# Six units instead of five with combined blocks in both layers, and another order of the attention work, in a fused attention and mixer kernel

## The chip, the cores and the metric

The kernel runs on one core of a Trainium2 chip. The metric is the device time of one execution in microseconds (us): the median of three runs before the change.

## What is computed

Eight batches of cosine attention with 12 heads, 448 positions and 64 elements per head, and then a mixer on the result. In the reference, cut to what matters:

```python
q_n = q / (norm(q) + 1e-6);  k_n = k / (norm(k) + 1e-6)
attn = softmax(q_n @ k_n.T / tau)            # per batch and head, 448 x 448
x = (attn @ v), heads side by side           # 8 x 448 x 768
h = (x.T @ U @ V).T                          # U: 448 x 32, V: 32 x 448, over positions
u = x + h
out = u + relu(u @ w_ch1) @ w_ch2            # w_ch1: 768 x 3072, w_ch2: 3072 x 768
```

Inputs and output are float32; the matmuls are bf16.

## The kernel before

**Attention.** For each batch, q and k come in three thirds of four heads by DMAs that POOL issues (L588). For each half third an engine squares the elements (L636 on ACT, L638 on POOL, L640 on DVE), DVE sums the squares (L644), ACT and DVE make the inverse norm (L658 to L666), and a normalizing product writes q or k of a pair of heads into a buffer (L712). Which engine does this product is `POOL_XN` (L351): POOL for q of batches 2 to 7, DVE for the rest. From batch 2 on a DMA on SP's queue transposes it (L728) into one of the `qkT` buffers; in batches 0 and 1 PE transposes (L566). Scores are computed in bursts of three slots (L774). Six slots of two PSUM banks hold up to 128 keys of two heads each; the last 64 keys of four heads share one slot, with four matmuls on a quarter of the array each. `groups_of` (L1491) puts slots into bursts, and `LAST` (L353) says at which head pair each of a batch's three quarter slots is placed. ACT takes the exponential of a slot (L792; L787 for the first raw keys), PE multiplies by v with a column of ones (L819, "values"), and DVE divides into X (L850 and L851; L855 and L857 in the first batches).

**Low rank.** After a batch, PE projects X by U (L934) and multiplies by V (L987), DVE adds the result to X (L996), and SP stores it as u in DRAM (L1025).

**Mixer.** The 28 tiles of 128 rows of u go through both layers in units: one of three tiles and one of one tile, plain (L1372 and L1414), and then twelve units of two tiles. In these twelve, the second layer is done in seven products of half blocks instead of eight (`mlp_seven`, L1248; its matmuls are L1289, 84 per unit), with blocks of w_ch2 that `seven_weights` has combined once, and sums of relu blocks by DVE (L1232 to L1234, `last_sums` L1243). The first layer of a unit is plain (L1260, 144 matmuls of 256 columns) for the first `HALF` = 7 of the twelve. The other five use seven products there too (`up_seven`, L1122; L1153, 252 matmuls of 128 columns, 36 per product). They need combined rows of w_ch1 (`seven_rows`, L1098, by DVE at L1112 to L1115, three of each), one of which is written over w_ch1 itself, and combined columns of u (L1135 to L1138). The row combinations lie in buffers of the attention that are free by then: X, `attn`, one v buffer, the buffers of normalized q and k. `up_seven` takes its products in the order 1, 6, 2, 7, 5, 3, 4; ACT copies product 1 (L1190), DVE adds sums from PSUM (L1175), ACT or DVE applies relu (L1181, L1209). One of its partial sums, `z12`, lies in a part of X (L445), so the copy waits until u of the last batches is stored (`x_free`).

**What sets the order.** Nothing is scheduled by hand. Every step is an `Op` with an engine, an estimated duration, what it depends on, buffers that it takes and releases, and a priority; some streams keep their order. `Plan.run` (L196) is a list scheduler over these estimates, and its order of starts is the program's order on each engine; at run time the engines wait for semaphores alone. An `Op` with `port=True` on DVE or POOL is not planned to start while one with `port=True` runs on the other. PE has the attention streams ahead of the mixer, whose matmuls fill what is left. At L1599 to L1602 the bursts of batches 3 to 7 get extra dependencies: the first of a batch on the last values matmul of the batch before, the second on L987 of the batch before, the fourth and later on values of an earlier pair of their own batch. In batch 0, where the plan has a gap on PE, warm-up matmuls (L698) are put in.

## Time and profile before

| what | us |
|---|---|
| median of three runs (lowest, highest) | 553.93 (553.42, 554.13) |
| the profiled execution, its own time | 553.89 |
| its span in the profile | 552.1 |
| first mixer matmul (L1372) | 39.16 |
| projections (L934) of batches 2 to 7 begin | 146.16, 193.88, 240.88, 286.89, 335.73, 379.80 |
| first combined first layer (L1153) begins | 409.06 |
| last matmul begins | 547.5 |

TensorE is called PE, VectorE DVE, ScalarE ACT, GpSimd POOL and SyncE SP. A line number such as L1289 is that of the kernel before. Busy time is time with an instruction on the engine; the table of groups gives the mean duration of one instruction, and the idle time of its engine just before it. The stretches cut the span into pieces; the chain of waits goes back from the last instruction to what released each step. The granted clock of PE is full but for one stretch of 3.4 us from about 20.6 us on.

### The profile page before, as it was taken

The numbers are of one execution on the slowest core, as the hardware profiler recorded it, in microseconds if no ns is written. First come the engines' busy times: TensorE is split into PE (matmuls) and PEld (weight loads), VectorE is DVE, ScalarE is ACT, GpSimd is POOL, SyncE is SP. The second block draws the span as 40 slices with busy tenths as digits, with TensorE's granted clock in tenths as the row PEclk, the third lists the DMA queues.
The fourth block names the chain that finished last, engine by engine and source line by source line (L and its number), as shares of the span: only waits on it lengthen the run. The fifth ranks groups of instructions, "written<-read, shape, count | busy, mean of one in ns | idle before, by whom it ended". The sixth has DMA issues, their size and how long they took to land.

```text
span 552.1 us, 14798 instructions
## 1 busy us (share of the span) xinstructions
PE 542.2 (98%) x6085; PEld 390.2 (71%) x6086; DVE 435.1 (79%) x978; ACT 281.4 (51%) x458; POOL 184.0 (33%) x216
## 2 busy tenths in 40 slices
PE   8899999999999999999999999999999999999996
PEld 6565565577857857767767767767778787878784
DVE  8889969989978897798789859657658585858583
ACT  7875746475575656656745754743314141414140
POOL 8626235325533552851543381020101111111111
PEclk9899999999999999999999999999999999999999
DMA  9999999959586949977997494332231312121201
GB/s 147 200 206 144 204 204 148 205 96 139 75 175 108 136 80 172 118 121 160 100 159 135 73 147 102 71 59 60 63 87 31 87 30 87 32 86 30 87 4 57
DMA packets 142324, 61.08 MB, mean 111 GB/s; under 512 B 101008, under 2 KB 142256, under 8 KB 142256
## 3 DMA queue, kind: packets, MB, share of 16 engines
q0 software_dynamic: 72352, 25.73, 43.0%
q1 hardware_dynamic: 69904, 34.41, 29.0%
q8 instruction: 47, 0.77, 0.6%
q14 instruction: 21, 0.17, 0.1%
HBM read 56.93 MB, written 15.93 MB: 132 GB/s over the span
## 4 chain that ended last, share of the span: by engine, by line
PE 91%; DVE 6%; ACT 1%; issue 1%; DMA 1%; DVEq 0%
PE bank L1289 30%; PE bank L1260 20%; PE bank L1153 13%; PE bank L819 8%; PE bank L774 7%; PE bank L1372 6%; PE bank L1414 4%; DVE qk_all L712 2%; PE bank L987 1%; DVE ss L644 1%; ACT attn L787 1%; PE bank L566 1%; PE bank L934 1%; DVE X_sb L857 1%; DMA relu<-in_q_dram 1%
## 5 line engine op out<-in xcount | busy, mean ns | idle before, releaser
L792 ACT ACTIVATE attn<-bank 128x896 bf16<-128x896 f32 (+1 forms) x163 | 140.4, 916 | 44.3 <-PE bank L774 43.8
L1289 PEld LDWEIGHTS <-relu 128*128 128x128 bf16 x1008 | 95.7, 98 | 66.4 <-issue 7.1
L1260 PE MATMUL bank<-uT,w_sb 128*128 128x256 bf16 x1008 | 120.2, 273 | 0.0
L1260 PEld LDWEIGHTS <-w_sb 128*128 128x128 bf16 x1008 | 95.2, 98 | 20.0 <-issue 7.9
L1289 PE MATMUL bank<-w_sb,relu 128*128 128x384 bf16 x576 | 102.7, 326 | 0.0
L712 POOL TENSOR_TENSOR qk_all<-qk_all,inv 112x512 bf16<-112x512 bf16 x36 | 41.0, 1148 | 85.0 <-DMA sqk<-qk_all 39.0
L644 DVE TENSOR_REDUCE ss<-sqk 112x8 f32<-112x512 bf16 x96 | 62.5, 672 | 4.4 <-ACT sqk L636 4.1
L819 PEld LDWEIGHTS <-attn 128*128 128x128 bf16 (+1 forms) x1536 | 55.1, 98 | 7.7 <-issue 4.2
L819 PE MATMUL bank<-v_nat,attn 128*128 128x65 bf16 (+1 forms) x1536 | 58.1, 194 | 0.9 <-DVE X_sb L857 0.4
L1270 ACT ACTIVATE relu<-bank 128x512 bf16<-128x512 f32 x53 | 31.6, 597 | 44.0 <-PE bank L1260 43.8
L774 PE MATMUL bank<-sqk 64*128 64x448 bf16 (+1 forms) x384 | 48.8, 359 | 1.1 <-ACT sqk L1436 0.5
L636 ACT ACTIVATE sqk<-qk_all 112x512 bf16<-112x512 bf16 x56 | 33.8, 632 | 23.3 <-DVE ss L644 22.0
L712 DVE TENSOR_TENSOR qk_all<-qk_all,inv 112x512 bf16<-112x512 bf16 x57 | 45.4, 821 | 0.3
L1153 PEld LDWEIGHTS <-w_sb 128*128 128x128 bf16 x720 | 41.0, 98 | 0.6
L1314 POOL TENSOR_TENSOR relu<-relu,u_nat 128x384 f32<-128x384 f32 x8 | 9.5, 1182 | 91.4 <-ACT relu L1312 91.3
L1190 ACT COPY attn<-bank 128x512 f32<-128x512 f32 x15 | 8.8, 585 | 60.4 <-PE bank L1153 59.5
L611 POOL DMA_DIRECT2D v_nat<-in_v_dram x42 | 31.2, 748 | 15.1 <-DMA w_sb<-in_moe_w_ch_dram 11.8
L1372 PE MATMUL bank<-uT,w_sb 128*128 128x384 bf16 (+1 forms) x288 | 35.6, 273 | 0.0
L1414 PE MATMUL bank<-w_sb,relu 128*128 128x384 bf16 x192 | 35.3, 326 | 0.0
L851 DVE TENSOR_TENSOR X_sb<-bank,rd 128x256 bf16<-128x256 f32 x72 | 30.5, 424 | 2.5
L1307 DVE TENSOR_TENSOR O_sb<-bank,O_sb 128x384 f32<-128x384 f32 x35 | 19.2, 554 | 16.2 <-PE bank L1289 11.5
L1153 PE MATMUL bank<-uT,w_sb 128*128 128x128 bf16 x540 | 31.8, 219 | 0.0
(137 smaller groups left out, 820.0 us busy)
## 6 DMA issues: line engine op xcount, KB each, us to landing
qk_all<-in_q_dram POOLq DMA_DIRECT2D x23, 224.0 KB, 4.4
qk_all<-in_k_dram POOLq DMA_DIRECT2D x23, 224.0 KB, 6.5
u_nat<-u SPq DMA_DIRECT2D x25, 192.0 KB, 2.8
w_sb<-in_moe_w_ch_dram POOLq DMA_DIRECT2D x4, 1152.0 KB, 17.7
w_sb<-in_moe_w_ch_dram POOLq DMA_DIRECT2D x8, 576.0 KB, 15.8
u<-X_sb SPq DMA_DIRECT2D x22, 192.0 KB, 4.7
v_nat<-in_v_dram POOLq DMA_DIRECT2D x11, 168.0 KB, 7.8
out_dram<-O_sb SPq DMA_DIRECT2D x12, 144.0 KB, 2.1
```

The source lines that it names most:

```text
L636: nc.scalar.activation(out=y, in_=x, func=AF.Square)
L644: lambda i=i, a0=a0, a1=a1, sq=sq: nc.vector.reduce_sum(ss.tile[:, i, a0:a1, :].rearrange("p h c -> p (h c)"), sq.tile[:, 0:a1 - a0, :].re ...
L712: (nc.gpsimd if pool_ else nc.vector).tensor_mul(dst, src, sc)
L774: nc.tensor.matmul(out=out, lhsT=qkT.tile.rearrange("p b s -> p (b s)")[r, n0:n0 + w], rhs=qkT.tile[r, SC:2 * SC, :].rearrange("p c s -> p ...
L792: exps.append(plan.add(Op("ACT", act_t(2 * S, 0.08), lambda sc=sc, c=c, attn=attn: nc.scalar.activation(out=attn.tile[:, :, off:off + S] i ...
L819: nc.tensor.matmul(out=av.tile[:, t, 0:D + 1], lhsT=tail.tile[:, hh, 128 * t:128 * (t + 1)] if tail and j == SC - 1 else (attn if j < SC - ...
L1153: o = plan.add(Op("PE", pe_t(128), lambda i=i, j=j, jj=jj: nc.tensor.matmul(out=mm.tile[:, 128 * jj:128 * jj + 128], lhsT=left[k](i, j), r ...
L1260: o = plan.add(Op("PE", pe_t(256), lambda j=j, e=e, cc=cc, mm=mm: nc.tensor.matmul(out=mm.tile[:, 256 * e:256 * e + 256], lhsT=w1_sb[:, cc ...
L1270: nc.scalar.activation(out=dst, in_=mm.tile[:, 0:512], func=AF.Relu)
L1289: o = plan.add(Op("PE", pe_t(CH), lambda j=j: nc.tensor.matmul(out=mm.tile[:, 0:CH], lhsT=left[k](j), rhs=right[k](j), start=(first and j ...
L1372: o = plan.add(Op("PE", pe_t(n), lambda cc=cc: nc.tensor.matmul(out=mm.tile[:, m:m + n], lhsT=w1_sb[:, cc, f * 128:(f + 1) * 128], rhs=uT. ...
L1414: nc.tensor.matmul(out=mm.tile[:, 0:c1 - c0], lhsT=relu.tile[:, f, i * 128:(i + 1) * 128], rhs=w2_t[:, f, c0:c1], start=(f == 0), stop=(f ...
```

## The change

- `HALF` is 6: the seventh of the twelve units does its first layer in seven products too, so six units do so.
- `LAST` has one placing for all batches from 2 on: a batch's three quarter slots go to head pairs 0, 2 and 4, so that three bursts hold one each. Before, batches 3 to 7 had two in the first burst and one in another.
- The first and second bursts of batches 4 to 7 have no extra dependency; batch 3 keeps them.
- q of batches 5 to 7 is normalized on DVE instead of POOL. Every normalizing product on DVE is now `port=True`, and the estimates of POOL's squares and products are 1.02 and 1.05 instead of 1.3 and 1.2.
- One of the twelve row combinations of w_ch1 (the third `S4`) goes to POOL.
- `z12` lies in `qkT` buffers instead of X. The copy of product 1 waits for the last values of batch 7, and the sum into `z12` for batch 7's last burst; neither waits for the stores of u.

The order in which the instructions stand after the change has 1512 matmuls at L1153 (1260 before), 864 at L1260 (1008), 147 warm-up matmuls (142), and otherwise the same matmuls. Normalizing products: 76 on DVE (58 before), 18 on POOL (36). ACT has 6 squares fewer and 4 relus of L1270 fewer, DVE 6 squares more and 8 relus of L1272 fewer. The diff, cut to its core:

```diff
-    HALF = 7
-    POOL_XN = {x: (0,) for x in range(2, B)}
+    HALF = 6
+    POOL_XN = {2:(0,),3:(0,),4:(0,)}
-    LAST = {0: 0, 2: 2, 4: 4}, {0: 0, 2: 0, 4: 4}
+    LAST = {0: 0, 2: 2, 4: 4}
...
-    xs, vs_ = X_t.bitcast(FP), v_t[1].rearrange("p h c d -> p (h c d)").bitcast(FP)
+    zs, vs_ = sqk_t[:, 3 * SQ + 2 * 2 * SC * SCH:].bitcast(FP), v_t[1].rearrange("p h c d -> p (h c d)").bitcast(FP)
-    r_z12 = fixed_ring([xs[:, 512 * i:512 * (i + 1)] for i in range(3, 6)])
+    r_z12 = fixed_ring([zs[:, 512 * i:512 * (i + 1)] for i in range(3)])
...
+    pool_s = plan.stream("POOL")
...
-                o = Op(on, 1.3 if on == "POOL" else 0.48 if on == "ACT" else 0.44, None,
+                o = Op(on, 1.02 if on == "POOL" else 0.48 if on == "ACT" else 0.44, None,
...
-            return plan.add(Op("POOL" if pool_ else "DVE", 1.2 if pool_ else dve_t(512), fn, deps=[deps[i]], acq=[xn],
-                               rel=[getattr(ld, "slot", ld), inv], prio=pr, port=pool_), pool_x if pool_ else None)
+            return plan.add(Op("POOL" if pool_ else "DVE", 1.05 if pool_ else dve_t(512), fn, deps=[deps[i]], acq=[xn],
+                               rel=[getattr(ld, "slot", ld), inv], prio=pr, port=True), pool_x if pool_ else None)
...
-        def rows_(f, deps, prio=2.5):
-            return plan.add(Op("DVE", 0.15 + N * 0.00053, f, deps=deps, prio=prio, port=True))
+        def rows_(f, deps, prio=2.5, eng="DVE"):
+            e = nc.gpsimd if eng == "POOL" else nc.vector
+            return plan.add(Op(eng, N * 0.00203 if eng == "POOL" else 0.15 + N * 0.00053, lambda: f(e), deps=deps, prio=prio,
+                               port=True), pool_s if eng == "POOL" else None)
-            a = rows_(lambda o=S1[i], x=A21, y=A22: nc.vector.tensor_add(o, x, y), free[i])
-            c = rows_(lambda o=S2[i], x=S1[i], y=A11: nc.vector.tensor_sub(o, x, y), [a, *free[3 + i]])
-            d = rows_(lambda o=S4[i], x=A12, y=S2[i]: nc.vector.tensor_sub(o, x, y), [c, *free[2]], 3)
-            e = rows_(lambda o=A21, x=A11, y=A21: nc.vector.tensor_sub(o, x, y), [a, *after], 2.7)
+            a = rows_(lambda v, o=S1[i], x=A21, y=A22: v.tensor_add(o, x, y), free[i])
+            c = rows_(lambda v, o=S2[i], x=S1[i], y=A11: v.tensor_sub(o, x, y), [a, *free[3 + i]])
+            d = rows_(lambda v, o=S4[i], x=A12, y=S2[i]: v.tensor_sub(o, x, y), [c, *free[2]], 3, "POOL" if i in (2,) else "DVE")
+            e = rows_(lambda v, o=A21, x=A11, y=A21: v.tensor_sub(o, x, y), [a, *after], 2.7)
-    def up_seven(tiles, relu, tops, ready, left, made_by, qk_free, x_free):
+    def up_seven(tiles, relu, tops, ready, left, made_by, qk_free, s_free, z_free):
...
-                                 [o, *x_free], [s1[g]])
+                                 [o, *s_free], [s1[g]])
-                    x["z12"] = op("DVE", PS, sum_op(of(z12[g]), of(s1[g]), B_, False), [o, x["cp"]], [z12[g]])
+                    x["z12"] = op("DVE", PS, sum_op(of(z12[g]), of(s1[g]), B_, False), [o, x["cp"], *z_free], [z12[g]])
...
-                slots += [(x, SC - 1) for x, at in LAST[b > TB].items() if at == p]
+                slots += [(x, SC - 1) for x, at in LAST.items() if at == p]
...
-            up = *up, [o for p in range(NPAIR) for o in got[B - 1, p, "qkT"][1]], [o for t in range(7) for o in made[3, t]]
+            up = *up, [o for p in range(NPAIR) for o in got[B - 1, p, "qkT"][1]], [last_av[B - 1, p] for p in range(NPAIR)], bursts[B - 1][-1:]
-            o.deps += ([last_av[b - 1, NPAIR - 1]] if k == 0 else first_v[b - 1] if k == 1 else
-                       [last_av[b, k - 3]] if k > 2 else [])
+            o.deps += ([last_av[b, k - 3]] if k > 2 else [] if b > 3 else
+                       first_v[b - 1] if k == 1 else [last_av[b - 1, NPAIR - 1]] if k == 0 else [])
```

## The prediction

> **What bounds the kernel now.** I read the page first, then the stretches of 20 us, the chain of waits, the timelines of TensorE (PE) and VectorE (DVE), and last the order in which both programs' instructions stand.

> ```profile
> PE 542.2 (98%) x6085; PEld 390.2 (71%) x6086; DVE 435.1 (79%) x978; ACT 281.4 (51%) x458; POOL 184.0 (33%) x216
> ```
> PE is busy 98% of the span, but its ends are modelled, so the stretches must say where it loses time.

> ```profile
> 0.00:20.00 20.00, 16.72 (x179) 12.21 (x179) 16.79 (x43) 15.14 (x33) 16.87 (x25) 1.00 1.37 160
> 20.00:40.00 20.00, 18.92 (x295) 12.93 (x294) 17.17 (x58) 17.36 (x26) 7.15 (x10) 0.91 1.23 207
> ...
> 80.00:100.00 20.00, 19.04 (x177) 11.04 (x178) 16.41 (x35) 12.11 (x22) 12.13 (x15) 1.00 1.35 148
> ...
> 280.00:300.00 20.00, 20.00 (x201) 13.19 (x199) 18.50 (x39) 8.73 (x15) 7.21 (x8) 1.00 0.74 128
> ```
> The columns are PE, weight loads, DVE, ACT, POOL. PE idles in the first 40 us (batch 0), about 1 us near 95 us, and then hardly at all; DVE is the next engine, with up to 18.5 us of 20.

> ```profile
> 384.88 10.70 PE bank L1260 x98
> 395.58 13.65 PE bank L1289 x84
> 409.23 14.07 PE bank L1153 x252
> 423.30 13.65 PE bank L1289 x84
> ```
> This is the chain of waits: nothing but PE, and each unit's price can be read. A combined first layer (L1153) is 252 matmuls in 14.07 us, 55.8 ns each; a plain one (L1260) runs at 10.70/98 = 109.2 ns, so its 144 take 15.72 us; a second layer (L1289) takes 13.65 us. From 384.9 us to the last matmul at 547.8 us these pieces meet without a gap.

> [...] the normalizing product on DVE (L712) takes 0.68 us alone and up to 1.53 us beside one on POOL.

> **The change, part by part.**

> *A sixth combined unit.* The order shows 252 L1153 matmuls six times instead of five, and 144 L1260 fewer. 15.72 - 14.07 = 1.65 us less PE work, on the path. Added with it are 15 bank sums on DVE (L1175, 0.69 us) and 9 relus (L1181, 0.62) and 3 copies (L1190, 0.585) on ACT. Today's five such units hide the same work without a gap, so it costs 0; without that cover PE would wait for its banks.

> *Quarter-array slots.* A burst of scores is three slots. Timeline of PE:

> ```profile
> 340.96 0.86 PE L774 MATMUL bank<-sqk 64*128 64x448 bf16 x10
> 341.76 2.03 PE L1260 MATMUL bank<-uT,w_sb 128*128 128x256 bf16 x17
> ...
> 346.77 0.74 PE L774 MATMUL bank<-sqk 64*128 64x448 bf16 x6
> 347.45 1.26 PE L1260 MATMUL bank<-uT,w_sb 128*128 128x256 bf16 x10
> ```
> From its start to the next line's a mixed burst (10 matmuls, one half-array slot and two quarter ones) takes 0.80 us, an unmixed one (6) 0.68: 0.12 us for the change of tile, and the one with a single quarter slot (8 matmuls, 361.68 to 362.47) 0.79, so the price is per mixed burst. Batches 3 to 7 have two mixed bursts now and three after: 5 x 0.124 = +0.62 us, on the path.

> *Order of the work.* With the first bursts of batches 4 to 7 tied to nothing, the order puts two bursts of the next batch ahead of the projections of the one before. Counting units from 1, the last attention matmul stood just inside the seventh unit's first layer (378 us); now it stands 48 matmuls before the end of the sixth unit's second layer, 48 x 0.1625 = 7.8 us ahead of the first combined layer, which is the seventh unit's. This moves PE work, it removes none. Does a moved burst find its operands? They come by a transposing DMA on SP's queue (1.23 us to issue, 5.1 us median to landing, 8.5 at most). PE work that stands between such a DMA and the burst that reads it is at least 8.9 us before; after it is at least 9.7 (batch 2) and 12.3 for the others. I cost it at 0; without that cover, up to 8.5 us once per batch. SP's own queue has the same 36 transposes and stores in another order; nothing new waits there.

> *Row combinations ahead of the first combined unit.* They now follow the last attention closely. From its last matmul to the seventh unit's second product, the first to read a row combination, PE has 7.8 + projections 0.4 + eight L987 of 0.1625 (1.3) + the first product, 36 x 0.0558 (2.0) = 11.5 us. DVE's queue up to the last row sum that this product needs: two column sums (0.54), a head scaling (0.55), two row sums (2 x 0.87), a unit sum (0.475): 3.3 us, so 8 us of cover and a cost of 0. All that is queued on DVE in that stretch, with three more unit sums and two relu sums (3 x 0.475 + 2 x 0.47), eight additions to X (8 x 0.465) and two in-place row differences (2 x 0.87) comes to 3.3 + 7.8 = 11.1 us; the last of it is read by the fourth product, 4 us later. If DVE comes 5 us late there, PE waits some 0.5 us. One row difference (1536 columns) goes to POOL. No row shows it; the nearest, 512 columns on POOL in 1.04 us, gives an estimate of 3.1 us, from 1.04 (no dearer than 512) to 4.7 us (1.55 per 512 beside DVE). It is read by the sixth product, over 10 us after the unit begins: 0 at either end. The new homes only change what is waited for: ACT's copy L1190 waits for the last attention instead of the stores of u, DVE's first sum for the last burst. Both are over before the unit; behind them queue that unit's relus. Cost 0.

> *Normalizing products to DVE.* Batches 5 to 7: 18 products leave POOL (18 x 1.04 = 18.8 us) and join DVE. POOL's q and k loads then no longer stand behind them. On DVE records overlap:

> ```profile
> 249.37 1.47 DVE L996 TENSOR_TENSOR X_sb<-bank,X_sb 128x384 bf16<-128x384 f32 x3
> ...
> 251.70 1.26 DVE L644 TENSOR_REDUCE ss<-sqk 112x8 f32<-112x512 bf16 x2
> ```
> Two reductions of 0.67 us take 1.26, three additions of 0.54 take 1.47: each following one occupies 0.08 us less than its record. So a product occupies 0.60 us, 18 of them 10.8 us. Per stretch between the projections of one batch and the next (from the order's counts, records less 0.08 each): batch 3 to 4, DVE 37.4 us against 44.5 of PE; 4 to 5, 35.5 against 42.7; 5 to 6, 32.8 against 42.4. Today it is 34.4 of 47.0, 33.6 of 46.0, 35.9 of 48.8. DVE goes from 73% to 84%: hidden, if DVE can give up idle time. I take 0; unhidden, see the rival.

> *The start.* Correcting POOL's price for squares reorders batch 0. DVE now takes the last two squares' sums before it normalizes: the first normalizing product, at 17.17 today, must follow POOL's fourth square (ends 17.71) and one sum, to about 18.4. ACT then does four copies before its first wide exponential, so that starts at about 22.0 instead of 20.55.

> ```profile
> 20.55 1.72 ACT L792 ACTIVATE attn<-bank 112x896 bf16<-112x896 f32 x2
> 22.16 0.23 ACT L658 ACTIVATE ln<-ss 112x32 f32<-112x32 f32 x1
> 22.42 0.23 ACT L659 ACTIVATE ln<-ln 112x32 f32<-112x32 f32 x1
> 23.17 2.90 ACT L792 ACTIVATE attn<-bank 112x896 bf16<-112x896 f32 x3 [0.52 <-PE bank L774]
> 26.07 0.53 ACT L1436 COPY sqk<-bank 128x448 bf16<-128x448 bf16 x1
> ```
> But what interrupts the 16 exponentials today goes ahead of them or to DVE: two small ones with the wait behind them (23.17 - 22.16 = 1.0 us) and a copy (0.5); and the last two thirds' normalizing is over 3 us sooner, which frees the waits between 31 and 35 us (0.5). -2.0 + 1.4 = -0.6 us. Bounds: +1.4 if nothing is recovered, -1.5 if all waits go. The five more warm-up matmuls (142 to 147, 0.28 us) stand in waits. The waits near 92 to 102 us (0.70 us for DVE's X, some 1.7 with the smaller ones) stand in nearly the same order: 0, from -0.9 to +0.9.

> **Sum.** The profiled execution took 553.89 us: span 552.1 and 1.8 around it; it lies 0.04 under the median of 553.93. 553.89 - 1.65 + 0.62 - 0.6 = 552.26, so 552.3 us.

> **Rivals.**
> *The gain is spent at the edges* (no change): the start gives +0.4 instead of -0.6 and the first combined unit waits 0.5 us. For it: the saving on PE is 1.0 us net, no more than one wait, and the start's order is new. Against it: exponentials are what the start waits for, and ACT's stretch gets cleaner. 552.3 + 1.0 + 0.5 = 553.8 us.
> *DVE becomes the bound* (slower): from batch 3's projections to batch 6's PE waits for head scalings and normalizing. It decides from the point where DVE idles or is blocked over 44.5 - 37.4 = 7.1 us in the first stretch, 7.2 in the second, 9.6 in the third. Today that sum is 12.6 (47.0 - 34.4), of which 7.3 us is idle by the stretches[...]. If it keeps 9 us a stretch, PE loses 1.9 + 1.8 us: 552.3 + 3.7 = 556.0 us. For it: DVE's 18.5 of 20 us already today. Against it: the 18 products leave POOL, so POOL blocks less, and the idle is mostly lack of work.

> **How the numbers follow.** Forecast 552.3: 0.56, with its own range 550.8 to 552.8. No change, at 553.8: 0.23. DVE as the bound, at 556.0: 0.21. A measurement of this kernel can tell about 0.2%, 1.1 us, from no change. Faster 0.56, same 0.23, slower 0.21. The low end is the forecast with the start's and the 95 us stretch's better bounds taken partly (-0.9 and -0.6); the high end, 555.8, goes into the slow case until no more than 2 in 10 is left out.

> **What would show it.** L1153 x1512 and L1260 x864; mixed bursts of 8 matmuls only, three in each batch; 14.07 us before every second layer from the first combined unit on, with no gap ahead of it. DVE busy at 82 to 90% between the third and the sixth projections, with PE at 100% and no wait of PE for DVE, confirms the cover; PE waits for DVE's X or for bank releases there would make the slow rival right. The first MLP matmul (L1372), at 39.16 us today, should come near 38.6; later than 40 would refute my working of the start.

## The result, and the profile after

The changed kernel takes 552.95 us (median of 20 runs, 550.98 to 554.85) against 554.10 for the kernel before (20 runs, 553.29 to 555.12): a ratio of 0.9973, 95% interval 0.9965 to 0.9982, so faster by 0.27%. Its times lie in two groups, ten from 550.98 to 552.56 and ten from 553.35 to 554.85, and what parts them is the subject of half of what follows. The profiled execution below is of the slower group (its own time 553.73 us, span 551.9); a second one, of the faster group (551.07 us, span 549.3), is called the repeat.

Three lines of the kernel have new numbers that are needed here: the plain first layer L1260 is now L1263, the second layer L1289 is L1292, the combined first layer L1153 is L1156. The first line of the page after:

```profile
PE 540.4 (98%) x6199; PEld 389.2 (71%) x6199; DVE 448.3 (81%) x1009; ACT 284.1 (51%) x464; POOL 167.8 (30%) x199
```
PE is as full as before; DVE is busy 13 us longer. The same stretches of 20 us as in the prediction (PE, weight loads, DVE, ACT, POOL, then the granted clock):

```profile
0.00:20.00 20.00, 16.49 (x192) 12.13 (x193) 17.03 (x42) 15.36 (x34) 16.64 (x25) 1.00 1.38 163
20.00:40.00 20.00, 18.52 (x295) 12.42 (x293) 16.57 (x58) 17.63 (x27) 7.02 (x10) 1.00 1.23 207
80.00:100.00 20.00, 18.56 (x174) 10.80 (x173) 18.27 (x38) 11.68 (x22) 10.02 (x13) 1.00 1.33 139
280.00:300.00 20.00, 20.00 (x199) 12.46 (x197) 17.08 (x39) 11.90 (x20) 4.46 (x6) 1.00 0.92 145
```
Two things differ. Between 20 and 40 us the granted clock is 1.00, not 0.91. And between 80 and 100 us PE is busy 0.48 us less than before, with DVE nearly 2 us busier. In the repeat the same stretch has 19.88:

```profile
80.00:100.00 20.00, 19.88 (x185) 11.69 (x183) 18.20 (x43) 11.29 (x24) 11.95 (x15) 1.00 1.31 164
```
The chain of waits at the end of the kernel after:

```profile
381.35 14.07 PE bank L1156 x252
395.42 13.65 PE bank L1292 x84
409.07 14.07 PE bank L1156 x252
...
519.95 14.07 PE bank L1156 x252
534.02 13.66 PE bank L1292 x84
```
Six combined units, each 14.07 + 13.65 us, without a gap.

To see where the time went I split PE's way into four parts. A stall is what lies between the starts of two successive matmuls beyond the first one's price (55.8 ns for 128 columns, in proportion), where that is over 0.15 us; the rest is called work, small pauses included. All in us:

| | before | after | repeat |
|---|---|---|---|
| start of the first channel-mixing matmul (L1372, now L1375) | 39.16 | 38.25 | 37.33 |
| work from there to the first combined unit | 367.61 | 339.37 | 339.36 |
| stalls in that part | 2.29 | 3.57 | 1.83 |
| of these between 85 and 105 us | 1.77 | 2.00 | 0.28 |
| combined units, to the start of the last matmul | 138.44 | 166.16 | 166.16 |
| start of the last matmul (the sum) | 547.50 | 547.35 | 544.68 |

So against before: after has 0.91 less at the start, 0.52 less work (28.24 less, and one combined unit of 27.72 more) and 1.28 more stalls, 0.15 less in all; the repeat has 1.83, 0.53 and 0.46 less, 2.82 in all. The work is the same in both groups. They differ in the start, by 0.92, and near 90 us, by 1.72. Of the 0.92, 0.67 lie ahead of the first scores, which begin at 8.21 us in the kernel after and at 7.54 in the repeat (7.74 before).

Near 90 us the trace tells why. The batches are numbered from 0, so the third batch is batch 2. Timelines of DVE and then of POOL, kernel after:

```profile
87.42 3.61 DVE L713 TENSOR_TENSOR qk_all<-qk_all,inv 112x512 bf16<-112x512 bf16 x2
```
```profile
88.41 2.05 POOL L713 TENSOR_TENSOR qk_all<-qk_all,inv 112x512 bf16<-112x512 bf16 x2
```
The same two in the repeat:

```profile
86.61 1.28 DVE L713 TENSOR_TENSOR qk_all<-qk_all,inv 112x512 bf16<-112x512 bf16 x2
```
```profile
88.02 2.06 POOL L713 TENSOR_TENSOR qk_all<-qk_all,inv 112x512 bf16<-112x512 bf16 x2
```
These are normalizing products of the third batch, two on each engine. In the kernel after DVE's second one starts at 88.02 us and is still running when POOL starts its pair at 88.41; it ends only after that pair, having taken 3.01 us and not 0.68. In the repeat DVE is through 0.14 us before POOL starts. On DVE head scalings of batch 1 are queued behind these products. PE waits for them in the kernel after (first) and does not in the repeat (second):

```profile
90.67 1.62 PE L1417 MATMUL bank<-w_sb,relu 128*128 128x384 bf16 x9
93.73 0.65 PE L820 MATMUL bank<-v_nat,attn 128*128 128x65 bf16 x16 [1.44 <-DVE X_sb L858]
```
```profile
89.75 1.62 PE L1417 MATMUL bank<-w_sb,relu 128*128 128x384 bf16 x9
91.21 0.65 PE L820 MATMUL bank<-v_nat,attn 128*128 128x65 bf16 x16
```

### The profile page after: what moved, and what is told of

It is laid out like the page before. It is cut to its first block, busy times and chain, and to the rows that moved or that the text cites. A ratio compares the mean times of both kernels' runs of the same rounds, so it can differ in the third digit from the quotient of the medians.

```text
span 551.9 us, 15023 instructions
## 1 busy us (share of the span) xinstructions
PE 540.4 (98%) x6199; PEld 389.2 (71%) x6199; DVE 448.3 (81%) x1009; ACT 284.1 (51%) x464; POOL 167.8 (30%) x199
## 4 chain that ended last, share of the span: by engine, by line
PE 88%; DVE 8%; DMA 1%; issue 1%; POOL 1%; ACT 1%; DVEq 0%; POOLq 0%
PE bank L1292 29%; PE bank L1263 17%; PE bank L1156 15%; PE bank L820 8%; PE bank L775 7%; PE bank L1375 6%; PE bank L1417 3%; DVE ss L645 2%; DVE qk_all L713 2%; PE bank L988 1%; DMA qk_all<-in_k_dram 1%; DVE X_sb L997 1%; PE bank L935 1%; PE bank L567 1%; DVE X_sb L858 1%
## 5 line engine op out<-in xcount | busy, mean ns | idle before, releaser
L1292 PEld LDWEIGHTS <-relu 128*128 128x128 bf16 x1008 | 95.8, 98 | 66.5 <-issue 6.4
L1263 PE MATMUL bank<-uT,w_sb 128*128 128x256 bf16 x864 | 104.0, 273 | 0.0
L1292 PE MATMUL bank<-w_sb,relu 128*128 128x384 bf16 x576 | 102.9, 326 | 0.2 <-DVE relu L1246 0.2
L1263 PEld LDWEIGHTS <-w_sb 128*128 128x128 bf16 x864 | 81.6, 98 | 17.4 <-issue 7.0
L713 DVE TENSOR_TENSOR qk_all<-qk_all,inv 112x512 bf16<-112x512 bf16 x75 | 52.6, 727 | 0.2
L1273 ACT ACTIVATE relu<-bank 128x512 bf16<-128x512 f32 x49 | 29.2, 596 | 41.7 <-PE bank L1263 38.9
L1156 PEld LDWEIGHTS <-w_sb 128*128 128x128 bf16 x864 | 49.2, 98 | 0.8
L1193 ACT COPY attn<-bank 128x512 f32<-128x512 f32 x18 | 10.6, 586 | 67.6 <-PE bank L1156 66.6
L589 POOL DMA_DIRECT2D qk_all<-in_q_dram x24 | 17.8, 740 | 84.4 <-DVE qk_all L713 26.6
L637 ACT ACTIVATE sqk<-qk_all 112x512 bf16<-112x512 bf16 x50 | 30.1, 634 | 18.0 <-DVE ss L645 18.0
L1156 PE MATMUL bank<-uT,w_sb 128*128 128x128 bf16 x648 | 38.1, 219 | 0.0
L1184 ACT ACTIVATE relu<-relu 128x512 bf16<-128x512 bf16 x36 | 22.7, 630 | 29.8 <-DVE relu L1178 28.8
L1375 PE MATMUL bank<-uT,w_sb 128*128 128x384 bf16 (+1 forms) x288 | 35.6, 273 | 0.0
L713 POOL TENSOR_TENSOR qk_all<-qk_all,inv 112x512 bf16<-112x512 bf16 x18 | 20.0, 1120 | 39.7 <-DMA sqk<-qk_all 25.1
```

Of the source, the lines that this page charges most:

```text
L713: (nc.gpsimd if pool_ else nc.vector).tensor_mul(dst, src, sc)
L1156: o = plan.add(Op("PE", pe_t(128), lambda i=i, j=j, jj=jj: nc.tensor.matmul(out=mm.tile[:, 128 * jj:128 * jj + 128], lhsT=left[k](i, j), r ...
L1263: o = plan.add(Op("PE", pe_t(256), lambda j=j, e=e, cc=cc, mm=mm: nc.tensor.matmul(out=mm.tile[:, 256 * e:256 * e + 256], lhsT=w1_sb[:, cc ...
L1292: o = plan.add(Op("PE", pe_t(CH), lambda j=j: nc.tensor.matmul(out=mm.tile[:, 0:CH], lhsT=left[k](j), rhs=right[k](j), start=(first and j ...
L1375: o = plan.add(Op("PE", pe_t(n), lambda cc=cc: nc.tensor.matmul(out=mm.tile[:, m:m + n], lhsT=w1_sb[:, cc, f * 128:(f + 1) * 128], rhs=uT. ...
```

## The experiments

My theory after this: the sixth unit carries the gain; the other parts make room for it; and the two groups come from POOL's pair holding DVE's. Rivals: DVE's greater load is what costs; or the groups come from the first landings alone. The start was open: I took it to be the new price of POOL's squares.

**The changed kernel again**, as it is.

> The changed kernel once more, for a second profile. Its 20 times fall into two groups, 551.0 to 552.6 us and 553.3 to 554.9 us; the kernel before has one group. Theory 1 (DVE blocked by POOL): in the first profile the second of two normalizing products on DVE at 87.4 us was held for 2.9 us by two products of POOL, and PE then waited 1.6 us near 92 us; whether they meet depends on when POOL's DMAs let it go, so a profile of the fast group shows no long product there, a wait of PE under 0.5 us, and a time some 1.5 us lower. Theory 2 (the start): the groups come from the first 40 us, where PE's granted clock may or may not drop, and the wait near 92 us is the same in both.

551.64 us (9 runs, 551.06 to 554.16), ratio 0.9955, interval 0.994 to 0.997. Its profile is the repeat shown above: of the faster group, DVE's pair 1.28 us, no wait at 91 us. The blocking and the wait come and go together in these two profiles. The clock does not part the groups: in all 29 executions of the changed kernel, of either group, the mean granted clock is 0.998 or more, and 3.4 us at half clock would bring it to 0.997.

**Five combined units** and all else as changed.

```
-    HALF = 6
+    HALF = 7
```

> The changed kernel with the seventh unit's first layer plain again (HALF = 7), all else as changed: one part undone. My theory (the sixth combined unit is worth its PE work, 1.65 us, and nothing waits at it): 1.65 us slower than the changed kernel, 554.6 us, thus no faster than before. Rival (the gain of the change comes from the new order and the start, and the unit's saving is spent on waits for its row combinations): within 0.5 us of the changed kernel.

555.04 us (14 runs, 553.51 to 556.01), ratio 1.0008 (0.9995 to 1.0021): the whole gain is gone. Its times too fall in two groups, six from 553.51 to 554.40 us and eight from 555.03 to 556.01; by their middles, 553.6 and 555.4, each lies 1.7 us above the changed kernel's (551.9 and 553.7), which is the price of the unit. Its profile is of the slower group, with a stall of 1.80 us near 92 us, and shows one wait more. From the list of PE's waits:

```profile
PE bank L820 <- DVE X_sb L858: 2.3, 3, 1.6
...
PE bank L1292 <- DVE relu L1236: 0.7, 1, 0.7
```
The last line is a wait at 539.9 us, ahead of the last second layer. So the sixth unit carries the gain.

**The kernel before with a sixth combined unit** and nothing else.

```
-    HALF = 7
+    HALF = 6
```

> The kernel before with HALF = 6 alone: six combined units without the freed bursts, the spread slots and the new home of z12. My theory (the other parts are what makes the sixth unit possible: its rows and its buffers come free too late without them): PE waits at the first combined unit, whose first copy and product-6 sum wait for the stores of u of the last batch (DMA landing 2 to 5 us after the additions); 2 to 5 us lost there, 554.5 to 557.5 us. Rival (the unit alone carries the gain): 554.1 - 1.65 = 552.4 us, with no wait at its first combined layer.

557.85 us (6 runs, 557.39 to 559.34), ratio 1.0066 (1.0048 to 1.0084). Alone, the unit makes the kernel 3.7 us slower, since it now begins while batch 7 is still being added up:

```profile
PE bank L987 <- DVE X_sb L996: 1.3, 1, 1.3
...
PE bank L1289 <- DVE relu L1233: 0.8, 1, 0.8
PE bank L1153 <- DVE X_sb L996: 0.7, 1, 0.7
```
The wait that I expected, for the stores of u, is the smaller part: PE waits 0.60 us at 391.6 us behind a sum of DVE that itself waited 0.81 us for a store. The rest stands behind row sums and additions to X on DVE. The other parts of the change, together, are worth about nothing by themselves (the run before this one) and are what makes the unit worth something.

**The placing of the quarter-array slots back.**

```
-    LAST = {0: 0, 2: 2, 4: 4}
+    LAST = {0: 0, 2: 2, 4: 4}, {0: 0, 2: 0, 4: 4}
...
-                slots += [(x, SC - 1) for x, at in LAST.items() if at == p]
+                slots += [(x, SC - 1) for x, at in LAST[b > TB].items() if at == p]
```

> The changed kernel with the old placing of the quarter slots for batches 3 to 7: two mixed bursts per batch instead of three. On PE that is 5 x 0.124 = 0.62 us less. But the order then puts the last scores and values inside the first combined unit, whose rows need the buffers of the last values. My theory: PE waits 2 to 4 us there, 554 to 556.5 us; the new placing pays for itself by ending the attention sooner. Rival (the placing is only a cost of 0.62 us): 552.3 us.

556.24 us (7 runs, 554.86 to 557.56), ratio 1.0040 (1.0024 to 1.0056). The five mixed bursts that this spares are paid for dearly: the order now puts the last attention inside the first combined layer. Timeline of PE:

```profile
376.18 0.90 PE L775 MATMUL bank<-sqk 64*128 64x448 bf16 x6
377.63 0.49 PE L1156 MATMUL bank<-uT,w_sb 128*128 128x128 bf16 x6 [0.56 <-ACT attn L793]
...
382.39 1.03 PE L988 MATMUL bank<-A_sb,V_sb 128*128 128x384 bf16 x4 [0.43 <-ACT A_sb L1439]
384.23 0.23 PE L1156 MATMUL bank<-qk_all,attn 128*128 128x128 bf16 x1 [0.80 <-DVE attn L1116]
```
PE stalls some 4.4 us between 376 and 386 us, for attention, additions and row sums that the changed kernel has behind it by then. From 385.2 us on it then runs at half clock for 3.4 us, which comes on top (mean granted clock of the execution 0.997).

**POOL's old price for squares back.**

```
-                o = Op(on, 1.02 if on == "POOL" else 0.48 if on == "ACT" else 0.44, None,
+                o = Op(on, 1.3 if on == "POOL" else 0.48 if on == "ACT" else 0.44, None,
```

> The changed kernel with the old estimate of 1.3 us for POOL's squares, all else as changed: the reordering of batch 0 undone. My theory (the start is worth 0.6 us as predicted, 0.9 as profiled): the first mixer matmul comes at 39.1 us again, not at 38.2 or 37.5. With DVE that much later at 87 us its pair of products meets POOL's in every run, so 1.6 us more: 554.0 us, one group. The order also puts projections inside the first combined unit; if that unit waits for its rows, 1 to 3 us on top. Rival (the start's gain is absorbed before 100 us): 553.0 us, no different from the changed kernel.

554.77 us (19 runs, 553.76 to 556.01), ratio 1.0015 (1.0008 to 1.0022). The first mixing matmul came at 38.42 us and not at 39.1: most of the start is not the price's. From the first score it took 30.34 us, against 30.03 in the kernel after, 29.79 in the repeat and 31.42 before. This order has no wait of 1.6 us near 92 us, but three of 0.76 to 1.05 between 108 and 119. The start did not move as expected, and that led to the next two runs.

**The kernel before with eleven idle matmuls more.** The prediction's own line for 20 to 40 us had a granted clock of 0.91, and I had made nothing of it. Within it the kernel before has this stretch:

```profile
20.60:24.00 3.40, 3.35 (x42) 2.39 (x40) 2.48 (x8) 2.84 (x5) 2.84 (x4) 0.50 1.16 210
```
PE at half clock for 3.4 us. Ahead of it the kernel before leaves PE idle for 0.82 us at 17.5 to 18.3 us; the changed order has eleven idle matmuls just there. My guess was that the gap brings the half clock, so I put eleven into the kernel before:

```
...
+        if o.by == "PE" and scored[0] == 8:
+            warm_up(11)
+            scored[0] = 9
         if o.by == "PE" and not cool:
...
```

> The kernel before, unchanged but for eleven idle matmuls put into the gap that its PE leaves at 17.5 to 18.3 us, ahead of the key transposes. In its profile PE then ran at half the granted clock for 3.4 us from about 20.6 us; the changed kernel, which has eleven idle matmuls at that place by its planner's choice, shows the full clock throughout. Theory: the shorter start of the changed kernel is this clock, not the earlier squares. Then this kernel shows no stretch below full clock after 8 us, its first mixer matmul comes 1.0 to 1.5 us sooner after the first score than in the kernel before, and the whole takes 552.6 to 553.2 us (1.0 to 1.5 less than before). Rival: the start is bound by the engines that normalize (DVE, ACT), and the clock of PE does not matter: no more than 0.3 us change.

553.83 us (21 runs, 552.60 to 555.16), ratio 0.9992 (0.9985 to 0.9998). The first half came as expected. Timeline of PE, then the same stretch:

```profile
16.81 0.68 PE L776 MATMUL bank<-sqk 64*128 64x448 bf16 x2
17.41 0.79 PE L698 MATMUL bank<-warm 128*128 128x128 bf16 x11
18.30 0.37 PE L566 MATMUL bank<-ident,qk_all 112*128 112x112 bf16 x4
```
```profile
20.60:24.00 3.40, 3.30 (x65) 2.46 (x64) 3.33 (x11) 3.37 (x6) 2.58 (x4) 1.00 1.16 210
```
Full clock, 65 matmul records where there were 42, and from 13.8 us up to there the two traces agree within 0.03 us. From the first score to the first projection onto U takes 26.74 us, against 28.17 before. All 21 executions have a mean granted clock of 0.998 or more. The kernel before itself agrees: of 104 executions beside these experiments, 81 have 0.997 or less, and 16 have 0.999 or more, which leaves no room for such a stretch. These 16 are 0.5 us shorter by the medians (553.74 and 554.25 us). So the half clock comes in most executions of that order, not in all.

The second half of what I expected did not come: only 0.46 us of the 1.43 reached the end by the medians (and nothing in the profiled execution, 554.27 us, one of the slower ones). What DVE and POOL do at 88 us:

```profile
88.27 3.54 DVE L712 TENSOR_TENSOR qk_all<-qk_all,inv 112x512 bf16<-112x512 bf16 x2
```
```profile
88.59 2.06 POOL L712 TENSOR_TENSOR qk_all<-qk_all,inv 112x512 bf16<-112x512 bf16 x2
```
In the kernel before DVE's pair comes later, when POOL's second product is just starting (its pair from 88.74 us):

```profile
89.82 2.12 DVE L712 TENSOR_TENSOR qk_all<-qk_all,inv 112x512 bf16<-112x512 bf16 x2
```
With the idle matmuls it is 1.5 us sooner and meets both of POOL's, and PE stalls 1.69 us at 91 us where it stalled 0.27.

**Both planning figures of the start back** (the squares' price, and DVE's normalizing products without `port=True`), which gives PE's old order up to 68 us.

```
-                o = Op(on, 1.02 if on == "POOL" else 0.48 if on == "ACT" else 0.44, None,
+                o = Op(on, 1.3 if on == "POOL" else 0.48 if on == "ACT" else 0.44, None,
...
-                               rel=[getattr(ld, "slot", ld), inv], prio=pr, port=True), pool_x if pool_ else None)
+                               rel=[getattr(ld, "slot", ld), inv], prio=pr, port=pool_), pool_x if pool_ else None)
```

> The changed kernel with the planner told, as in the kernel before, 1.3 us for a square on POOL[...]. Its order of PE over the first 68 us is then that of the kernel before. Theory: these two planning figures are the part of the change that set the new order of the start; with them back, the stretch at half clock returns (3.4 us from about 20.6 us) and the first mixer matmul is 1.0 to 1.5 us later after the first score. The new order also puts some of the last projections among the first combined unit's matmuls, which brought waits of 3 us and more in other orders; so 554.5 to 558 us. Rival: the half clock was chance of one execution: full clock, first mixer matmul as in the changed kernel.

565.32 us (6 runs, 564.35 to 569.90), ratio 1.0189 (1.0175 to 1.0202): much slower than expected. In its profile, of the slowest of the six executions, PE stalls some 18 us in all after the start, in an order that is new from about 110 us on. What it was made for came:

```profile
20.60:24.00 3.40, 3.40 (x44) 2.25 (x40) 2.39 (x8) 2.51 (x5) 2.44 (x4) 0.57 1.16 210
```
The half clock is back with the old order of the start, and it comes twice more in this profile, from 163.5 and from 405.8 us on, each time behind waits of PE (mean granted clock of the execution 0.989, against 0.997 in the kernel before). From the first score to the first projection: 28.17 before, 28.11 in the run with the sixth unit alone, 27.56 here; and with full clock 26.92 after, 26.67 in the repeat, 26.74 in the kernel before with idle matmuls. Why this run lies 0.6 us under the other two at half clock stays open.

**The third batch's products on DVE as well**, so that POOL has none at 88 us.

```
-    POOL_XN = {2:(0,),3:(0,),4:(0,)}
+    POOL_XN = {3:(0,),4:(0,)}
```

> The changed kernel with batch 2's normalizing products of q on DVE too, so that POOL has no product to run before batch 3's (POOL_XN for batches 3 and 4 alone). Theory 1 (blocking by POOL near 88 us costs PE 1.6 us in the slow group): the wait near 92 us goes, the times make one group at 551.5 us or below. Rival (DVE simply has too much work there): six more products of 0.6 us on DVE make the wait longer, 553 to 555 us.

555.42 us (19 runs, 553.58 to 557.77), ratio 1.0026 (1.0014 to 1.0037). The wait near 92 us is gone, as expected; but the planner made a new order, with the first combined layer begun among batch 7's projections, and its row sums stand behind additions to X:

```profile
384.70 0.23 PE L1156 MATMUL bank<-uT,w_sb 128*128 128x128 bf16 x1 [0.22 <-DVE w_sb L1118]
386.96 2.07 PE L1156 MATMUL bank<-uT,w_sb 128*128 128x128 bf16 x34 [2.03 <-DVE w_sb L1118]
```
The profiled execution (553.93 us) kept full clock. Of the 19, 12 have a mean granted clock of 0.997 or less, and these are 1.4 us longer by the medians (556.05 and 554.64 us). The times tell nothing of the two groups.

**All of q's products from the third batch on, on POOL again.**

```
-    POOL_XN = {2:(0,),3:(0,),4:(0,)}
+    POOL_XN = {x: (0,) for x in range(2, B)}
```

> The changed kernel with q of batches 5 to 7 normalized on POOL again. My theory (18 products more on DVE are hidden, DVE has room): no gain, 552 to 554 us, and PE without waits between 150 and 340 us in both; DVE 13 us less busy. Rival (DVE was at its limit in the changed kernel): faster than it, 551 us or below, with less waiting of PE for DVE between 150 and 340 us.

558.30 us (4 runs, 556.76 to 559.36), ratio 1.0065 (1.0044 to 1.0085). Between 150 and 340 us PE stalls 0.23 us, against 1.19 in the changed kernel. So the 18 products on DVE cost 1 us there at most, and probably less: the run with the old price for squares has them on DVE too and stalls 0.19 us. What costs is again the first combined unit, with 5.2 us of waits and, among them, a stretch of 3.4 us at half clock (mean granted clock of the execution 0.995), and there POOL holds DVE. Timelines of DVE and POOL:

```profile
385.33 4.71 DVE L1118 TENSOR_TENSOR w_sb<-w_sb 128x1536 bf16<-128x1536 bf16 x2
```
```profile
384.71 3.64 POOL L1117 TENSOR_TENSOR attn<-w_sb,attn 128x1536 bf16<-128x1536 bf16 x1 [18.76 <-DVE attn L1116]
```
The first of DVE's two in-place differences takes 3.84 us and not 0.95.

**POOL's first product of the third batch made to follow DVE's second, in the plan.**

```
+        if b == 2 and h0 == 0:
+            pairs[0][1].deps.append(pairs[-1][0])
```

> The changed kernel with one more dependency: in batch 2's first third, POOL's first normalizing product waits for the third's second product on DVE, so that POOL can't take the pair of DVE products near 87 us. Theory 1 (the two groups of times are DVE's pair before or behind POOL's pair): one group, at 551.5 us, without a wait of PE over 0.5 us near 92 us. Rival (the groups come from elsewhere, or the planner's new order brings a wait of its own): still two groups, or 553 us and more. The order puts the last additions to X directly ahead of the first combined unit, so a wait there of up to 1 us can come on top in either case.

561.16 us (4 runs, 560.36 to 561.74), ratio 1.0125 (1.0111 to 1.0139). It failed in two ways. The tie moved the plan only: POOL waits on data, and there was none to wait on, so the two pairs met again (DVE 3.05 us, POOL 2.52) and PE waited 1.04 us at 91.8. And the new plan had waits of its own, 3.9 us at the first combined unit, with 6.8 us at half clock behind them (mean granted clock of the execution 0.994), and 1.5 at 324 us. It tells nothing of what parts the two groups.

**The same by data, in the changed kernel's own order.** Ahead of POOL's first product stands a copy of two columns that DVE's second one wrote. The rest of the edit finds POOL's two products and puts them behind DVE's second one in the program.

```
...
+    def held_():
+        nc.gpsimd.tensor_copy(hold_t, xn_.tile[:, 0, 0:2])
+        first_()
+    late[0].fn = held_
...
```

> The changed kernel in its own order, with one small copy on POOL (two columns, of what the DVE's second normalizing product of the third batch wrote) ahead of POOL's first product of that batch, so that POOL cannot start before DVE is through. Theory: the two groups of times come from POOL's two products at 88 us, which in the slower group start before the DVE's product is through and hold it for up to 3 us; held back by 0.3 us at most, they cannot. Then the times lie in one group at 551.0 to 552.3 us, DVE's pair takes about 1.3 us, and PE has no wait over 0.5 us near 92 us. Rival: the groups come from the time of the first landings alone: two groups as before, 551.0 to 554.9.

552.12 us (5 runs, 551.21 to 552.86), ratio 0.9956 (0.9943 to 0.9968): one group, none in the slower one. But five executions are few: of the changed kernel's 29, 18 are in the faster group, so five in a row would come by chance about one time in ten. DVE, then POOL:

```profile
86.73 1.28 DVE L714 TENSOR_TENSOR qk_all<-qk_all,inv 112x512 bf16<-112x512 bf16 x2
```
```profile
88.07 0.18 POOL L1618 COPY hold<-qk_all 112x2 bf16<-112x2 bf16 x1 [0.67 <-DVE qk_all L714]
88.21 2.04 POOL L714 TENSOR_TENSOR qk_all<-qk_all,inv 112x512 bf16<-112x512 bf16 x2
```
POOL now waits 0.67 us for DVE: it was ready at 87.4 us, just after DVE's second product had started, so without the copy the two would have met in this execution. PE has 0.57 us of stalls between 85 and 105 us. Against the kernel before this is the same as the repeat's 0.9955; that it beats the changed kernel's 0.9973 may come from the lack of a slower group, but the intervals overlap and do not show it.

**The row difference on DVE, in the changed kernel's own order.**

```
-            e = nc.gpsimd if eng == "POOL" else nc.vector
+            e = nc.vector
```

> The changed kernel in its own order, with the third difference of the rows for the combined layer on DVE and not on POOL. Theory, as forecast: POOL's 3.3 us lie beside other work and nothing waits for it; on DVE the same operation takes about 0.95 us and comes at 375 us, where DVE is already late with the additions to X. The changed kernel has no gap before the first combined unit but 0.35 us at 379.7; with 0.95 us more on DVE a wait of 0.3 to 1.0 us appears there: 552.0 to 554 us, 0.3 to 1.0 above the changed kernel's middle. Rival: POOL's difference blocks DVE there, and taking it away makes DVE sooner: as the changed kernel or up to 0.5 us less.

553.04 us (22 runs, 551.77 to 557.42), ratio 0.9984 (0.9973 to 0.9996). Lines of DVE, then of PE:

```profile
374.76 0.95 DVE L1117 TENSOR_TENSOR attn<-w_sb,attn 128x1536 bf16<-128x1536 bf16 x1
375.74 2.80 DVE L997 TENSOR_TENSOR X_sb<-bank,X_sb 64x384 bf16<-64x384 f32 x5
```
```profile
376.94 0.32 PE L988 MATMUL bank<-A_sb,V_sb 128*128 128x384 bf16 x1 [0.27 <-DVE X_sb L997]
```
With 0.95 us more ahead of the additions to X, PE stalls 1.22 us between 376 and 379 us where the changed kernel has 0.35. The difference of 0.87 lies in the expected 0.3 to 1.0; on POOL the operation is hidden and on DVE it is not. This is read from the profile: the median is 0.1 us above the first of the changed kernel's two and 1.4 above the second, which by itself shows nothing.

Not tried: the old ties of the bursts, or the old home of `z12`, with the rest as changed. What these two parts are worth alone stays open.

## Why the prediction came out

The direction is right and the number is close: 552.3 forecast, 552.95 and 551.64 the two medians. The unit's term is right for its reason; that the whole sum came so near is partly luck, because other terms were wrong and offset each other. In us, against the kernel before:

| term of the sum | forecast | after | repeat |
|---|---|---|---|
| sixth combined unit | -1.65 | -1.66 | -1.66 |
| mixed bursts | +0.62 | +0.62 | +0.62 |
| all other work (small pauses of PE) | 0 | +0.52 | +0.51 |
| start | -0.6 | -0.91 | -1.83 |
| waits between 85 and 105 us | 0 | +0.23 | -1.49 |
| all other stalls | 0 | +1.05 | +1.03 |
| sum | -1.63 | -0.15 | -2.82 |

*The sixth unit.* Right in mechanism and size. Plain first layers give back 15.86 us, second layers 13.52, and a combined unit of 27.72 comes: 1.66. Its sums and relus are hidden, as costed. Taken away, the gain is gone.

*Mixed bursts.* Right in count and size. From its start to the next line's, a mixed burst takes 0.80 us and an unmixed one 0.67 in the kernel before, after and in the repeat, wherever it stands from batch 2 on (only two unmixed ones of the changed kernel take 0.75).

*All other work.* This had no term in the forecast. Of the 0.52 us, 0.28 lie in the second layers of the first two units, between 71 and 128 us, and 0.34 in the matmuls by U and V (one record of these is missing before, so this is unsure). They are pauses of less than 0.15 us each; what makes them longer is not shown.

*The start.* The sign was right, the reason wrong, and that is luck. What I worked out of ACT came true: the first wide exponential starts at 21.90 us (about 22.0 forecast), and eight then run on without a break:

```profile
21.90 6.84 ACT L793 ACTIVATE attn<-bank 112x896 bf16<-112x896 f32 x8
```
But this was not worth the time. The kernel before, in its own order and with ACT interrupted as ever, is as quick from the first score on, once PE keeps its clock (26.74 us against 26.92 and 26.67). The step that failed is "-2.0 + 1.4": the waits of ACT at 23.2 us and between 31 and 35 us, put down to the interruptions, came of a PE at half clock. The one of 0.52 us falls into the slow stretch; the one of 0.44 us, at 32.2, comes 8 us after it. In the kernel before with idle matmuls both are gone:

```profile
22.54 2.51 ACT L794 ACTIVATE attn<-bank 112x896 bf16<-112x896 f32 x3
24.94 0.54 ACT L1438 COPY sqk<-bank 128x448 bf16<-128x448 bf16 x1
25.35 4.23 ACT L794 ACTIVATE attn<-bank 112x896 bf16<-112x896 f32 x5
```
"The five more warm-up matmuls stand in waits", costed at nothing, was the place to look. That is also why the square's price alone mattered little.

*The waits near 92 to 102 us.* "Nearly the same order: 0, from -0.9 to +0.9" held for the kernel after and was mis-sized for the repeat, at -1.49; the same order met another timing. From the trace of the kernel before, the forecast had that a product of DVE takes up to 1.53 us and not 0.68 beside one of POOL's. What this costs changes with the times at which the two start (DVE's pair takes 3.61 us in the kernel after and 1.28 in the repeat), and these the forecast did not follow. Six profiles:

| | DVE's pair starts | POOL's pair starts | DVE's pair takes | PE's stalls, 85 to 105 us |
|---|---|---|---|---|
| before | 89.82 | 88.74 | 2.12 | 1.77 |
| before with idle matmuls | 88.27 | 88.59 | 3.54 | 3.19 |
| after | 87.42 | 88.41 | 3.61 | 2.00 |
| repeat | 86.61 | 88.02 | 1.28 | 0.28 |
| POOL held by data | 86.73 | 88.21 | 1.28 | 0.57 |
| row difference on DVE | 87.14 | 89.08 | 1.28 | 1.04 |

DVE's pair comes sooner as the start gets shorter. POOL's moves less, since ahead of it in POOL's queue stand DMA issues that wait for earlier landings (0.49, 0.64 and 0.67 us in the kernel after). So an earlier DVE first pays more and then nothing, and 0.9 us between two starts became 2.7 us at the end. That POOL's products hold DVE's is seen wherever a pair here takes more than 1.28 us, and the run that holds POOL back by data agrees. That the hold is what parts the two groups rests on one profile of each and on that run's five executions; that the start alone sets into which group an execution falls is read from these profiles and not tested.

*Costed at nothing.* DVE's cover held. Between the projections of batches 3, 4, 5 and 6:

```profile
208.39:253.46 45.07, 45.00 (x500) 31.42 (x499) 40.04 (x95) 28.43 (x46) 14.31 (x19) 1.00 0.96 129
253.46:296.41 42.95, 42.94 (x485) 29.97 (x485) 37.11 (x92) 28.18 (x46) 13.83 (x19) 1.00 1.09 133
296.41:339.65 43.24, 42.92 (x482) 29.79 (x481) 36.58 (x88) 27.38 (x43) 11.29 (x15) 1.00 0.90 124
```
DVE is busy 85 to 89%, PE 99 to 100%: the rival of DVE as the bound is refuted. DVE is busy 1.6 to 3.8 us a stretch longer than forecast (37.4, 35.5 and 32.8), and even that is hidden. POOL's row difference took 3.28 us (3.1 estimated) and is hidden; moved bursts found their operands. What was missed is small: six stalls of 0.17 to 0.35 us after 205 us, 1.57 in all, where the kernel before has two of 0.52 in all, at 200 to 202 us. One of the six stands just ahead of the first combined unit:

```profile
379.04 0.98 PE L1292 MATMUL bank<-w_sb,relu 128*128 128x384 bf16 x5
380.20 1.15 PE L1292 MATMUL bank<-w_sb,relu 128*128 128x384 bf16 x6 [0.19 <-DVE relu L1246]
381.19 2.17 PE L1156 MATMUL bank<-uT,w_sb 128*128 128x128 bf16 x36
```
I had said there would be none. There the margin is thinner than the 8 us of cover that I worked out: 0.95 us more on DVE made 0.87 us more of stalls, for the additions to X and the last sums, which the forecast had not followed as waits of their own.

*The rival of a gain spent at the edges* came true in part, in the slower group: 0.15 us is left of 1.66. But it was neither the start nor the first combined unit that spent it. The start gave 0.9 us, more than forecast; the mixed bursts took what was forecast, and pauses, small stalls and the wait near 92 us took 1.8 us that the forecast had at nothing.

## What to carry to other kernels

Where an engine's granted clock is below full in one stretch, ask first what the engine did in the 3 or 4 us ahead of it; eleven idle matmuls in a gap of 0.8 us made the start 1.4 us shorter, as much as the reordering of the whole start did, though here only a third of it reached the end. Time won early is kept only if what comes later moves with it: an engine whose queue waits for landings can stay nearly where it is (with the idle matmuls POOL's pair came 0.15 us sooner, DVE's 1.55), and a faster neighbour can then run into it. In a planned kernel, test one part in the unchanged order, and by data rather than by a tie in the plan, since a new plan brought waits of 3 to 7 us, and in four of these runs stretches at half clock behind such waits, that say nothing about the part.

## What the hardware showed that I had not expected

A DVE product that was already running was held by POOL products that started 0.3 to 0.4 us after it, and through two of them on end: 3.01 us and 2.93 us for 0.68 (kernel after; kernel before with idle matmuls). But DVE does not always lose. In the fourteen profiles of this case an arithmetic instruction of POOL starts during 54 normalizing products of DVE that began with none of POOL's under way (where two start, the first is meant). In 42 of these, DVE's product takes its usual 0.67 to 0.69 us; in 33 of them POOL's is a normalizing product that takes 1.33 to 1.82 us, for 1.04 alone (in the kernel before, DVE's from 243.58 us on takes 0.69 us and POOL's from 243.62 on 1.55). In the other 12, DVE's takes 0.98 to 3.21 us. In these 12 POOL's instruction follows directly on a DMA issue of POOL's, which in 11 was under way when DVE's product started; among the 42 that is so in only 8. So either engine can be the one that takes longer. Which it will be, the starts of the two records do not tell, and whether POOL's DMA issue ahead of its product counts is not tested.

An in-place difference of 1536 columns on DVE took 3.84 us for 0.95, beside one on POOL that had started 0.6 us earlier and took 3.64 (3.28 in the changed kernel).
